# Fused backward of a linear-attention and a grouped-KV attention block: dK and dV in two shared PSUM banks, dK on eight array tiles

## The chip, the core and the metric

One core of a Trainium2 chip runs the whole kernel in one launch. The metric is the device time of that launch in microseconds. Five engines work side by side, each through its own instructions in order: TensorE (PE, with its weight loads listed apart as PEld), VectorE (DVE), ScalarE (ACT), GpSimd (POOL) and SyncE (SP, which here only issues DMAs).

## The reference, cut to what matters

Two attention blocks, A (linear attention) and B (softmax attention with one key/value head shared by 16 query heads), run forward on 2048 tokens of width 448; their outputs are concatenated, and the gradients of all inputs are taken against `grad_out`. The change is in block B:

```python
q = (x @ wq).reshape(B, S, H, Dh).transpose(0, 2, 1, 3)     # 16 heads, Dh = 28
k = x @ wk ; v = x @ wv                                     # one head each
scores = einsum("bhqd,bkd->bhqk", q, k) * Dh ** -0.5
p = softmax(scores) ; o = einsum("bhqk,bkd->bhqd", p, v)
out = o.reshape(B, S, H * Dh) @ wo
```

Its backward needs, for each head, dV = pᵀ dO, dP = dO vᵀ, dS = p ∘ (dP − rowsum), dQ = dS k and dK = dSᵀ q. Since all heads share k and v, dK and dV are sums over all 16 heads and all 2048 queries: one accumulator each, open from the first block of queries to the last.

## The kernel before

Phase A computes block A forward and backward and projects block B's q, k and v. Then the core, which the change touches, does block B's attention forward and backward in one loop over units `u` (L905). Work is cut into 64 blocks `b` (a block is 256 queries of a pair of heads), each into 8 units `tp` (256 of the 2048 keys). A unit handles its 256 keys as two halves `t2`, two heads `h`. Stages of one block run at different lags behind each other, all written out by hand inside the loop, so the order on each engine is the order of the code. In what follows r is `u % 8`. Unit u issues:

- `rows_SD` (L663): the score matmuls S of unit u into two of three rotating score banks `SB`, and the dP matmuls of unit w = u − 16 into the two banks `DB`. Each matmul uses 32 rows and all 128 columns of the array (the form 32\*128), 256 columns of moving data, eight matmuls a unit. The four dP matmuls wait for the readers of the `DB` banks of the unit before.
- on ACT: exp of the first head's scores (L927), the copy `cp` of the second head's dP out of PSUM (L941), exp of the second head's scores (L973). On DVE: dS of the first head (L939) and, for unit u − 18, a 32x32-block transpose of dS into `dsx` (L1006). On POOL: dS of the second head from `cp` (L942).
- in even units, `o_dq`: 16 matmuls that accumulate o (unnormalised output) and dQ in the bank `oq` (form 128\*32: 128 rows, 32 columns, four side by side), around them the small work of a block (the output projection `out_proj` in r = 0, transposes `onat_T` in r = 2, `don_T` in r = 6), and `dv_mm` (L875): groups of four matmuls of 512 columns into `dv_acc`, one group in r = 2 and r = 6, two in r = 4.
- in odd units, `dk_m` (L840) four times: each is four matmuls on the four diagonal 32x32 tiles of the array, tile (32a, 32a), 512 columns each, into rows 32a of `dk_acc`. Row block `a` holds group `a` of every 128 keys (32 keys each), and nothing is summed across row blocks.

Every 4th unit SP issues a DMA transpose of the exponentials (L975), which `dv_mm` later reads.

PSUM has eight banks: three `SB`, one `dv_acc` (it takes the place of a phase-A bank from u = 1 on), two `DB`, `oq` and `dk_acc`. Until u = 25, `dk_acc` also serves the projection `do_proj`/`do_copy` (L882, L891) of `grad_out`. After the loop, `dv_acc` and `dk_acc` are copied to `dkvT` (L1023 to L1031), from which the pad rows (L1069), dK's and dV's projections and the gradients of wk and wv follow.

The PE order of an odd unit followed by an even one is thus S/dP, dK, S/dP, o/dQ (with dV), and each change of form is a change of the array's tiling.

Of the kernel before, what the change touches and what calls it, by code (L numbers as in the profile page):

```python
# [8 lines left out]
ACT = mybir.ActivationFunctionType  # L9
ALU = mybir.AluOpType  # L10
AX = mybir.AxisListType
BF16 = mybir.dt.bfloat16
F32 = mybir.dt.float32
# [4 lines left out]
P = 128  # L18
# [7 lines left out]
def kernel(  # L26
# [21 lines left out]
    nc = tc.nc  # L48
    S = A_x.shape[1]
    NS = S // P  # L50
    NQC = S // 512
    scale = float(DH) ** -0.5
# [27 lines left out]
    def mm(out_ap, lhsT, rhs, start=True, stop=True):  # L80
        nc.tensor.matmul(out_ap, lhsT=lhsT, rhs=rhs, start=start, stop=stop, tile_position=(0, 0))  # L81
# [521 lines left out]
    def q_shift(pn, shift, tmp):  # L603
        a = tmp[0][0:H, :]
        nc.scalar.activation(out=a, in_=pn[0:H, :], func=ACT.Identity, bias=eps[:, 0:1], scale=kmax2[:, 0:1])
        i32 = mybir.dt.int32
        nc.vector.tensor_scalar(out=a.bitcast(i32), in0=a.bitcast(i32), scalar1=1, scalar2=None, op0=ALU.logical_shift_right)
        nc.vector.tensor_scalar(out=shift, in0=a, scalar1=1.004 * 2.0 ** 63.5, scalar2=None, op0=ALU.mult)
# [10 lines left out]
    psA = psc.enter_context(tc.tile_pool(name="psA", bufs=4, space=bass.MemoryType.PSUM))  # L619
# [7 lines left out]
    NB = 64  # L627
    NU = NB * 8
    qT_B = [R1[:, g, :] for g in range(4)]
    vaug, kn, do_nat = vaug_, kn_, R2x[:, 0:NS, :]  # L630
    with ExitStack() as cs_:
# [8 lines left out]
        pp_ = cs_.enter_context(tc.tile_pool(name="cout", bufs=2, side="right"))  # L640
        SB = [psA.tile([P, 512], F32, name="aacc") for i in range(3)]
        DB = [psA.tile([P, 512], F32, name="agen") for i in range(2)]
        oq, dk_acc = (psA.tile([P, 512], F32, name="agen") for _ in range(2))

        dsT, dsx, qX, don, doT, rl, prod = ({} for _ in range(7))
        ETs = [pe_.tile([P, 4, 2, 512], BF16, name=f"eT{i}") for i in range(5)]
# [5 lines left out]
        def eN(b, c):  # L652
            return ENs[(2 * b + c // 2) % 6][:, 16 * (c % 2):16 * (c % 2) + 16, :]

        def mmt(out, lhsT, rhs, pos, start, stop):
            nc.tensor.matmul(out, lhsT=lhsT, rhs=rhs, start=start, stop=stop, tile_position=pos,  # L656
                             skip_group_check=True)

        def blk(b):
            qc, pair = divmod(b, 8)  # L660
            return qc, pair, pair // 2, pair % 2
# [26 lines left out]
        woTp, gbT = R4, R2.rearrange("p t (c k) -> p t c k", k=P)  # L688
# [151 lines left out]
        def dk_m(b, m):  # L840
            qc, pair, g, hp = blk(b)
            h, B, s = m // 8, (m // 2) % 4, m % 2
            for a in range(4):
                rhs = dsx[b][32 * a:32 * a + 32, :, h, :, :].rearrange(
                    "p u t (b i s) -> p u t b i s", b=4, s=2)[:, :, :, B, :, s]
                mmt(dk_acc[32 * a:32 * a + 32, :],
                    qX[qc][32 * a:32 * a + 32, B, s, pair * 64 + 32 * h:pair * 64 + 32 * h + 32],
                    rhs, (32 * a, 32 * a), b == 0 and m == 0, b == NB - 1 and m == 15)

        def o_mm(v):  # L850
            b, tp = divmod(v, 8)
# [16 lines left out]
        def o_dq(vs, ys):  # L868
            for v, y in zip(vs, ys):
                todo = [f(i) for f, i in ((o_mm, v), (dq_mm, y)) if 0 <= i < NU]  # L870
                for _ in range(2):
                    for g_ in todo:
                        next(g_)

        def dv_mm(dv_acc, b, h, qb):  # L875
            for c in range(4):
                rhs = eN(b, c).rearrange("p (u h t q) k -> p u h t q k", u=2, h=2,
                                                       t=2)[:, :, h, :, qb, :]
                mmt(dv_acc[32 * c:32 * c + 32, :], don[b][:, qb, h, :], rhs, (0, 32 * c),
                    b == 0 and h + qb == 0, b == NB - 1 and h + qb == 2)  # L880

        def do_proj(i, c0, c1, ps):  # L882
            for c in range(4):
                if c1 - c0 == 512:
                    mm(ps[:, :], gbT[:, i, c, :], woTp[:, c, :], start=(c == 0), stop=(c == 3))
                    continue
                for j in range(4):
                    js = slice(32 * j, 32 * j + 32)
                    mmt(ps[js, 0:c1 - c0], gbT[:, i, c, js], woTp[:, c, c0:c1], (0, 32 * j), c == 0, c == 3)

        def do_copy(i, c0, c1, ps):  # L891
            nc.vector.tensor_copy(out=do_nat[:, i, c0:c1], in_=ps[:, 0:c1 - c0])

        do_slots = {2 * i + 1: (i, 0, 512) for i in range(13)}
        do_slots.update({32 + 8 * n: (13 + n // 4, n % 4 * P, n % 4 * P + P) for n in range(12)})
        with tc.manual_schedule():
# [8 lines left out]
            for u in range(NU + 28):  # L905
# [3 lines left out]
                b0, b1, spare = ((SB[i] for i in ((0, 1, 2), (0, 2, 1), (1, 0, 2), (1, 2, 0))[u % 4]) if hasS else SB)  # L909
# [10 lines left out]
                    out_proj(*op, spare)  # L920
                dpj = do_slots.pop(u, None)
                if dpj is not None:
                    dps_ = DB[u // 2 % 2] if u < 16 else dk_acc if u < 27 else spare
                    do_proj(*dpj, dps_)

                if hasS:
# [1 line left out]
                if u == 1:  # L928
                    q_shift(pn3, shifts[3], [pd_.tile([P, 2, 512], BF16, name="dsT").rearrange("p a b -> p (a b)").bitcast(F32)
                                             for _ in range(1)])  # L930
                    dv_acc = psA.tile([P, 512], F32, name="aacc")
                if u == 11:
                    for n in (2, 3):
                        put_shift(nc.sync, shifts[n], slice(n * 512, n * 512 + 512))
# [21 lines left out]
                if (b := due(u, 27)) is not None:  # L956
                    qc, pair, g, hp = blk(b)
                    nc.vector.tensor_scalar(out=qT_B[g][64 * hp:64 * hp + 64, qc * 256:(qc + 1) * 256],  # L958
                                            in0=oq[64:128, 0:256], scalar1=scale, scalar2=None, op0=ALU.mult)
# [10 lines left out]
                if dpj is not None:  # L970
                    do_copy(*dpj, dps_)
# [8 lines left out]
                if u % 2:  # L980
                    b, i = divmod(u - 27, 8)
                    if 0 <= b < NB:
                        for m in range(2 * i, 2 * i + 4):
                            dk_m(b, m)
                else:
                    o_dq((u - 1,), (u - 19,))
                    b, n = divmod(u - 20, 8)
                    for k in {0: (0, 1), 2: (2,), 6: (3,)}.get(n, ()) if 0 <= b < NB else ():
                        dv_mm(dv_acc, b, k // 2, k % 2)
                y = u - 18  # L990

                if 512 <= u < 530 and u % 2 == 0:
# [9 lines left out]
                if 0 <= y < NU:  # L1002
                    b, tp = divmod(y, 8)
                    if tp == 0:
                        dsx[b] = px_.tile([P, 8, 2, 2, 256], BF16, name="dsx")
                    nc.vector.transpose(  # L1006
                        out=dsx[b][:, tp, :, :, :].rearrange("p h t c -> p (h t c)").bitcast(F32),
                        in_=dsT[y][:, :, :].rearrange("p h c -> p (h c)").bitcast(F32))

        dkvT, wqT, xb = post["dkvT"], post["wqT"], post["xb"]  # L1010
# [4 lines left out]
        def gen(i, dt=F32):  # L1015
            gens[i % 2] += 1
            t = [SB, DB][i % 2][gens[i % 2] % (3 - i % 2)]
            return t.bitcast(dt) if dt != F32 else t
# [2 lines left out]
            return pd_.tile([P, 2, 512], BF16, name="dsT")[:, 0, :]  # L1021

        for c in range(4):  # L1023
            nc.vector.tensor_copy(out=dkvT[32:64, c * 512:(c + 1) * 512], in_=dv_acc[32 * c:32 * c + 32, :])
        for c in range(4):
            t = dkvT[0:32, :].rearrange("p (t a i) -> p t a i", a=4, i=32)[:, :, c, :]
            src = dk_acc[32 * c:32 * c + 32, :].rearrange("p (t i) -> p t i", i=32)
            if c % 2:
                nc.vector.tensor_scalar(out=t, in0=src, scalar1=scale, scalar2=None, op0=ALU.mult)
            else:  # L1030
                nc.scalar.activation(out=t, in_=src, func=ACT.Copy, scale=scale)  # L1031

        def dwq(c):
            r = DC_ROWS[c]
# [44 lines left out]
        for c in range(4):  # L1079
            r = DC_ROWS[c]  # L1080
            ps = gen(0)
            for st in range(NS):
# [3 lines left out]
                                 func=ACT.Copy)  # L1086
# [35 lines left out]
```

## Time and profile before

| | us |
|---|---|
| median of three runs | 1066.51 (1065.31 to 1067.93) |
| profiled execution | 1067.99 |
| its span, first to last instruction | 1066.3 |
| first exp (L927) to last, 512 units | 220.0 to 990.6 |
| mean unit between u = 40 and u = 500 | 1.512 |

| engine | busy us | share of the span |
|---|---|---|
| PE | 1042.2 | 98% |
| DVE | 896.1 | 84% |
| ACT | 873.7 | 82% |
| POOL | 781.3 | 73% |

A row of a group names line, engine, operation, output and inputs by the program's names, their shapes, the count, then busy time in us, the mean of one in ns, and the engine's idle time before them. L656 is the line of the helper `mmt`, so its groups are told apart by the tiles: `agen<-dsx,qX` is dK, `aacc<-eN,don` is dV, `agen<-doT,R` is dP, `aacc<-R,R` 32\*128 is S, `agen<-eT,R` is o and `agen<-dsT,R` is dQ. A row of the timeline gives the start, the length from the first start to the last end of what it merges, and the count. The ends of matmuls are modelled, and matmuls overlap.

### The profile page before, as it was taken

The numbers are of one execution on the slowest core, as the hardware profiler recorded it, in microseconds if no ns is written. First come the engines' busy times: TensorE is split into PE (matmuls) and PEld (weight loads), VectorE is DVE, ScalarE is ACT, GpSimd is POOL, SyncE is SP. The second block draws the span as 40 slices with busy tenths as digits, with TensorE's granted clock in tenths as the row PEclk, the third lists the DMA queues.
The fourth block names the chain that finished last, engine by engine and source line by source line (L and its number), as shares of the span: only waits on it lengthen the run. The fifth ranks groups of instructions, "written<-read, shape, count | busy, mean of one in ns | idle before, by whom it ended". The sixth has DMA issues, their size and how long they took to land.

```text
span 1066.3 us, 39861 instructions
## 1 busy us (share of the span) xinstructions
PE 1042.2 (98%) x16241; PEld 476.1 (45%) x16241; DVE 896.1 (84%) x1797; ACT 873.7 (82%) x1741; POOL 781.3 (73%) x1033
## 2 busy tenths in 40 slices
PE   9999999999999999999999999999999999999998
PEld 5555555433444444444444444444444444444434
DVE  7888400459999999999999999999999999999943
ACT  6454122479999999999999999999999999999622
POOL 6001242227988898899889989988998999888881
PEclk9999999999999999999999999999999999999999
DMA  9749899079999999999999999999999999999963
GB/s 267 163 95 200 161 214 250 21 138 168 192 202 198 170 203 187 195 191 193 196 186 189 197 192 198 185 191 194 195 195 195 195 191 186 206 191 179 218 141 92
DMA packets 689936, 195.14 MB, mean 183 GB/s; under 512 B 670616, under 2 KB 687792, under 8 KB 689752
## 3 DMA queue, kind: packets, MB, share of 16 engines
q1 hardware_dynamic: 680152, 179.92, 99.2%
q0 software_dynamic: 4640, 8.71, 2.8%
q10 hardware_dynamic: 4960, 3.96, 1.3%
q8 instruction: 127, 2.08, 0.7%
q14 instruction: 57, 0.47, 0.1%
HBM read 12.60 MB, written 10.84 MB: 22 GB/s over the span
## 4 chain that ended last, share of the span: by engine, by line
PE 52%; DVE 35%; POOL 4%; issue 4%; ACT 3%; DMA 1%; DVEq 0%; POOLq 0%; ACTq 0%
PE agen L656 20%; PE agen L81 15%; DVE dsT L939 14%; DVE dsx L1006 12%; PE aacc L656 9%; PE aacc L81 7%; POOL dsT L942 4%; DVE R L958 2%; DVE oTs L801 2%; DVE oTs L955 2%; ACT cp L941 1%; DVE rl L800 1%; ACT eT L973 1%; DMA dsx<-R 1%; ACT eT L927 0%
## 5 line engine op out<-in xcount | busy, mean ns | idle before, releaser
L942 POOL TENSOR_TENSOR dsT<-cp,eT 128x512 bf16<-128x512 bf16 x512 | 588.1, 1157 | 77.3 <-ACT cp L941 68.9
L1006 DVE STREAM_TRANSPOSE dsx<-dsT 128x512 f32<-128x512 f32 x512 | 356.4, 696 | 2.4 <-POOL dsT L942 0.2
L656 PEld LDWEIGHTS <-R 32*128 32x128 bf16 (+1 forms) x9104 | 215.5, 93 | 318.3 <-issue 293.0
L939 DVE TENSOR_TENSOR dsT<-agen,eT 128x512 bf16<-128x512 f32 x512 | 338.5, 661 | 11.7 <-PE agen L656 8.4
L941 ACT ACTIVATE cp<-agen 128x512 bf16<-128x512 f32 x512 | 324.7, 634 | 12.5 <-PE agen L656 12.5
L927 ACT ACTIVATE eT<-aacc 128x512 bf16<-128x512 f32 x512 | 324.0, 633 | 11.6 <-PE aacc L656 4.7
L973 ACT ACTIVATE eT<-aacc 128x512 bf16<-128x512 f32 x512 | 330.6, 646 | 0.0
L656 PE MATMUL agen<-doT,R 32*128 32x256 bf16 x2048 | 270.9, 269 | 10.9 <-DVE dsT L939 8.2
L656 PE MATMUL aacc<-R,R 32*128 32x256 bf16 (+1 forms) x2240 | 269.7, 268 | 2.7 <-ACT eT L927 0.8
L656 PE MATMUL agen<-dsx,qX 32*32 32x512 bf16 x4096 | 267.7, 375 | 0.0
L656 PE MATMUL agen<-eT,R 128*32 128x256 bf16 x2048 | 182.0, 276 | 0.1
L656 PE MATMUL agen<-dsT,R 128*32 128x256 bf16 x2048 | 181.4, 276 | 0.1
L656 PEld LDWEIGHTS <-qX 32*32 32x32 bf16 x4096 | 79.7, 89 | 114.9 <-issue 54.3
L656 PE MATMUL aacc<-eN,don 128*32 128x512 bf16 x1024 | 97.6, 379 | 0.0
L81 PEld LDWEIGHTS <-R 128*128 128x128 bf16 (+1 forms) x517 | 41.0, 99 | 42.9 <-issue 11.1
L406 POOL COPY pk<-R 128x256 bf16<-128x256 bf16 x4 | 1.6, 397 | 75.3 <-DVE R L366 75.3
L81 PE MATMUL agen<-R,R 128*128 128x448 bf16 (+1 forms) x180 | 42.4, 363 | 0.3 <-ACT R L225 0.3
L833 POOL COPY qst<-R 128x512 bf16<-128x512 bf16 x56 | 34.2, 611 | 4.8 <-DMA qX<-qst 4.6
L805 POOL TENSOR_TENSOR prod<-R,oTs 128x128 f32<-128x128 bf16 x64 | 27.5, 430 | 9.8 <-DVE oTs L801 9.8
L656 PEld LDWEIGHTS <-don 128*32 128x32 bf16 x1024 | 34.2, 97 | 0.8
L422 DVE TENSOR_TENSOR osb<-aacc,pr 64x448 bf16<-64x448 f32 x2 | 1.2, 617 | 37.9 <-DMA out_dram<-osb 24.0
L958 DVE TENSOR_SCALAR R<-agen 64x256 bf16<-64x256 f32 x64 | 27.3, 426 | 3.6 <-PE agen L656 1.6
(231 smaller groups left out, 971.1 us busy)
## 6 DMA issues: line engine op xcount, KB each, us to landing
out_dram<-osb ACTq DMA_DIRECT2D x22, 112.0 KB
eN<-eT SPq DMA_TRANSPOSE x128
xa<-in_A_x_dram SPq DMA_DIRECT2D x8, 224.0 KB
ga<-in_grad_out_dram SPq DMA_DIRECT2D x4, 448.0 KB
xa<-in_grad_out_dram POOLq DMA_DIRECT2D x4, 448.0 KB, 5.7
out_dram<-wdq POOLq DMA_DIRECT2D x8, 224.0 KB, 3.8
eT<-in_grad_out_dram SPq DMA_DIRECT2D x4, 448.0 KB
eT<-in_B_x_dram SPq DMA_DIRECT2D x4, 448.0 KB
```

The lines of the kernel that those rows point to most:

```text
L81: nc.tensor.matmul(out_ap, lhsT=lhsT, rhs=rhs, start=start, stop=stop, tile_position=(0, 0))
L656: nc.tensor.matmul(out, lhsT=lhsT, rhs=rhs, start=start, stop=stop, tile_position=pos, skip_group_check=True)
L801: nc.vector.tensor_tensor(out=os_, in0=onp[:, :, :, :], in1=r_[:].to_broadcast([P, 2, 2, 32]), op=ALU.mult)
L805: nc.gpsimd.tensor_tensor(out=prod[b][:], in0=dnv, in1=os_, op=ALU.mult)
L833: eng.tensor_copy(out=st.rearrange("p (b s) a j -> p b s a j", s=2)[:, :, s, :, :], in_=src.unsqueeze(2).to_broadcast([P, 4, 4, 32]))
L927: nc.scalar.activation(out=eT(u)[:, 0, :], in_=sp[0][:, :], func=ACT.Exp, scale=scale)
L939: nc.vector.tensor_tensor(out=dst[:, 0, :], in0=dp[0][:, :], in1=ew[:, 0, :], op=ALU.mult)
L941: nc.scalar.activation(out=cp[:, :], in_=dp[1][:, :], func=ACT.Copy)
L942: nc.gpsimd.tensor_tensor(out=dst[:, 1, :], in0=cp[:, :], in1=ew[:, 1, :], op=ALU.mult)
L958: nc.vector.tensor_scalar(out=qT_B[g][64 * hp:64 * hp + 64, qc * 256:(qc + 1) * 256], in0=oq[64:128, 0:256], scalar1=scale, scalar2=None, ...
L973: nc.scalar.activation(out=eT(u)[:, 1, :], in_=sp[1][:, :], func=ACT.Exp, scale=scale)
L1006: nc.vector.transpose(out=dsx[b][:, tp, :, :, :].rearrange("p h t c -> p (h t c)").bitcast(F32), in_=dsT[y][:, :, :].rearrange("p h c -> p ...
```

## The change

dK and dV no longer have a bank each: both banks hold dK in columns 0 to 255 and dV in columns 256 to 511, each for half of the keys (n = 0, 1). A dK step issues eight matmuls of 256 columns in place of four of 512: for each row block `a`, one on tile (32a, 32a) into bank 0 and one on tile (32a, 32((a+1) mod 4)) into bank 1. A dV group becomes eight matmuls of 256 columns in place of four of 512. So that dK's accumulation can start without a clearing flag beside dV's, dV's first block (b = 0) is issued whole in u = 26, after the last `do_proj` in these banks; `do_proj` and `do_copy` of u = 17 to 25 work in two halves. The copies after the loop are 16 of 256 columns in place of 8 of 512. The order of everything else is as it was.

```diff
-        oq, dk_acc = (psA.tile([P, 512], F32, name="agen") for _ in range(2))
+        oq, acc0 = (psA.tile([P, 512], F32, name="agen") for _ in range(2))
+        kv_acc = [acc0]
...
             for a in range(4):
                 rhs = dsx[b][32 * a:32 * a + 32, :, h, :, :].rearrange(
                     "p u t (b i s) -> p u t b i s", b=4, s=2)[:, :, :, B, :, s]
-                mmt(dk_acc[32 * a:32 * a + 32, :],
-                    qX[qc][32 * a:32 * a + 32, B, s, pair * 64 + 32 * h:pair * 64 + 32 * h + 32],
-                    rhs, (32 * a, 32 * a), b == 0 and m == 0, b == NB - 1 and m == 15)
+                for n in range(2):
+                    j = 32 * ((a + n) % 4)
+                    mmt(kv_acc[n][j:j + 32, 0:256],
+                        qX[qc][32 * a:32 * a + 32, B, s, pair * 64 + 32 * h:pair * 64 + 32 * h + 32],
+                        rhs[:, 4 * n:4 * n + 4], (32 * a, j), False, b == NB - 1 and m == 15)
...
-        def dv_mm(dv_acc, b, h, qb):
-            for c in range(4):
...
-                mmt(dv_acc[32 * c:32 * c + 32, :], don[b][:, qb, h, :], rhs, (0, 32 * c),
-                    b == 0 and h + qb == 0, b == NB - 1 and h + qb == 2)
+        def dv_mm(b, h, qb):
+            for n in range(2):
+                for c in range(4):
+                    rhs = eN(b, c).rearrange("p (u h t q) k -> p u h t q k", u=2, h=2, t=2)[:, n, h, :, qb, :]
+                    mmt(kv_acc[n][32 * c:32 * c + 32, 256:512], don[b][:, qb, h, :], rhs, (0, 32 * c),
+                        b == 0 and h + qb == 0, b == NB - 1 and h + qb == 2)
...
-                    for k in {0: (0, 1), 2: (2,), 6: (3,)}.get(n, ()) if 0 <= b < NB else ():
-                        dv_mm(dv_acc, b, k // 2, k % 2)
+                    for k in ({0: (0, 1), 2: (2,), 6: (3,)} if b else {6: range(4)}).get(n, ()) if 0 <= b < NB else ():
+                        dv_mm(b, k // 2, k % 2)
...
         for c in range(4):
-            nc.vector.tensor_copy(out=dkvT[32:64, c * 512:(c + 1) * 512], in_=dv_acc[32 * c:32 * c + 32, :])
+            for n in range(2):
+                nc.vector.tensor_copy(out=dkvT[32:64, c * 512 + n * 256:c * 512 + n * 256 + 256],
+                                      in_=kv_acc[n][32 * c:32 * c + 32, 256:512])
```

More of the change, by code (lines that the diff above doesn't have):

```diff
@@ L873, in o_dq @@
                         next(g_)
-        def dv_mm(dv_acc, b, h, qb):
-            for c in range(4):
-                rhs = eN(b, c).rearrange("p (u h t q) k -> p u h t q k", u=2, h=2,
-                                                       t=2)[:, :, h, :, qb, :]
-                mmt(dv_acc[32 * c:32 * c + 32, :], don[b][:, qb, h, :], rhs, (0, 32 * c),
-                    b == 0 and h + qb == 0, b == NB - 1 and h + qb == 2)
-        def do_proj(i, c0, c1, ps):
+        def dv_mm(b, h, qb):
[4 more added lines that the diff above has]
+                        b == 0 and h + qb == 0, b == NB - 1 and h + qb == 2)
+        def do_proj(i, c0, c1, ps):
+            if ps is None:
+                for n in range(2):
+                    for c in range(4):
+                        mm(kv_acc[n][:, 0:256], gbT[:, i, c, :], woTp[:, c, 256 * n:256 * n + 256], start=(c == 0), stop=(c == 3))
+                return
             for c in range(4):
@@ L891, in do_copy @@
         def do_copy(i, c0, c1, ps):
+            if ps is None:
+                for n in range(2):
+                    nc.vector.tensor_copy(out=do_nat[:, i, 256 * n:256 * n + 256], in_=kv_acc[n][:, 0:256])
+                return
             nc.vector.tensor_copy(out=do_nat[:, i, c0:c1], in_=ps[:, 0:c1 - c0])
@@ L922 @@
                 if dpj is not None:
-                    dps_ = DB[u // 2 % 2] if u < 16 else dk_acc if u < 27 else spare
+                    dps_ = DB[u // 2 % 2] if u < 16 else None if u < 27 else spare
                     do_proj(*dpj, dps_)
@@ L930 @@
                                              for _ in range(1)])
-                    dv_acc = psA.tile([P, 512], F32, name="aacc")
+                    kv_acc.append(psA.tile([P, 512], F32, name="aacc"))
                 if u == 11:
@@ L1023 @@
         for c in range(4):
-            nc.vector.tensor_copy(out=dkvT[32:64, c * 512:(c + 1) * 512], in_=dv_acc[32 * c:32 * c + 32, :])
+            for n in range(2):
+                nc.vector.tensor_copy(out=dkvT[32:64, c * 512 + n * 256:c * 512 + n * 256 + 256],
+                                      in_=kv_acc[n][32 * c:32 * c + 32, 256:512])
         for c in range(4):
[L1026 to L1031, printed above, removed]
+            for n in range(2):
+                t = dkvT[0:32, n * S // 2:(n + 1) * S // 2].rearrange("p (t a i) -> p t a i", a=4, i=32)[:, :, c, :]
+                j = 32 * ((c + n) % 4)
+                src = kv_acc[n][j:j + 32, 0:256].rearrange("p (t i) -> p t i", i=32)
+                if c % 2:
+                    nc.vector.tensor_scalar(out=t, in0=src, scalar1=scale, scalar2=None, op0=ALU.mult)
+                else:
+                    nc.scalar.activation(out=t, in_=src, func=ACT.Copy, scale=scale)
         def dwq(c):
```

## The prediction, made before the changed kernel was run

> **What bounds the kernel now.** I read the engine table first, then the chain's shares, then the groups of the steady loop, and then the timeline of single units, which overturns the first two.
>
> ```profile
> PE 1042.2 (98%) x16241; PEld 476.1 (45%) x16241; DVE 896.1 (84%) x1797; ACT 873.7 (82%) x1741; POOL 781.3 (73%) x1033
> ...
> PE 52%; DVE 35%; POOL 4%; issue 4%; ACT 3%; DMA 1%; DVEq 0%; POOLq 0%; ACTq 0%
> ```
>
> PE looks like the bound: busy 98%, 52% of the chain. But ends of matmuls are modelled, and a PE that waits in the middle of a burst still counts as busy. The groups of the loop (300 to 1000 us, by form; 463 units):
>
> ```profile
> L1006 DVE STREAM_TRANSPOSE dsx<-dsT 128x512 f32<-128x512 f32 x463 | 322.3, 696 | 2.2 <-POOL dsT L942 0.2
> L939 DVE TENSOR_TENSOR dsT<-agen,eT 128x512 bf16<-128x512 f32 x463 | 306.0, 661 | 7.4 <-PE agen L656 4.3
> ...
> L941 ACT ACTIVATE cp<-agen 128x512 bf16<-128x512 f32 x463 | 294.5, 636 | 3.7 <-PE agen L656 3.6
> ...
> L656 PE MATMUL agen<-dsx,qX 32*32 32x512 bf16 x3700 | 241.9, 375 | 0.0
> ```
>
> ACT runs three operations a unit. They start 0.477 us apart, and without a pause each ends 12 to 13 ns later after its start than the one before, so ACT's real pace is 0.49 us: 1.47 us a unit, of a mean unit of 1.512. DVE has about 1.42 us of starts a unit. There is at most (1.512 − 1.47) x 512 = 21 us to gain, whatever PE does. Now the pair of units 249 (r = 1) and 250 (r = 2): PE's timeline, and of ACT's the copy `cp` of unit 249.
>
> ```profile
> 594.16 1.05 PE L656 MATMUL agen<-dsx,qX 32*32 32x512 bf16 x16
> 595.14 0.28 PE L656 MATMUL aacc<-R,R 32*128 32x256 bf16 x2
> 595.15 0.28 PE L656 MATMUL agen<-doT,R 32*128 32x256 bf16 x1
> 595.26 0.27 PE L656 MATMUL aacc<-R,R 32*128 32x256 bf16 x2
> 595.27 0.43 PE L656 MATMUL agen<-doT,R 32*128 32x256 bf16 x3
> 595.63 0.29 PE L656 MATMUL agen<-eT,R 128*32 128x256 bf16 x2
> ```
>
> ```profile
> 594.55 0.72 ACT L941 ACTIVATE cp<-agen 128x512 bf16<-128x512 f32 x1
> ```
>
> dK ends and S/dP of unit 250 start at 595.14. But the last two dP matmuls write the bank that `cp` of unit 249 reads until 594.550 + 0.725 = 595.275. The first starts 0.051 later, the second 0.108 after it, and the o/dQ phase 0.195 after that: 595.629, 0.354 after the end of `cp`. I took this distance for every even unit of some 60 blocks. It is 0.354 at the median for r = 0, 2, 4 and 6 alike; its mean lies above that by 0.003 (r = 0), 0.009 (2), 0.029 (4) and 0.000 (6). **So the end of `cp`, not the end of dK, starts nearly every o/dQ phase.** dK ends 0.136, 0.136, 0.020 and 0.095 before `cp` (medians). Since the waiting dP can issue 0.03 after S/dP starts, dK could be longer by 0.157, 0.157, 0.041 and 0.116 before o/dQ moved.
>
> What costs the 0.5 us a block in which ACT idles, then? Two loops without dK. From exp to exp, r = 1 to r = 3: `cp` starts 0.478 after the exp and takes 0.725; 0.354 to o/dQ; o/dQ with `onat_T` and a dV group lasts 1.148; the second S matmul 0.12 later, the exp 0.304 after it: 3.129, which is what the trace has (594.072 to 597.201; ACT alone needs 2.87). Then DVE's burst of small work, r = 1 to 4:
>
> ```profile
> 597.46 0.65 DVE L939 TENSOR_TENSOR dsT<-agen,eT 128x512 bf16<-128x512 f32 x1
> 598.14 0.42 DVE L958 TENSOR_SCALAR R<-agen 64x256 bf16<-64x256 f32 x1
> 598.49 0.70 DVE L1006 STREAM_TRANSPOSE dsx<-dsT 128x512 f32<-128x512 f32 x1
> 599.21 0.69 DVE L939 TENSOR_TENSOR dsT<-agen,eT 128x512 bf16<-128x512 f32 x1
> ```
>
> DVE has no pause here; the dP matmul of unit 253 waits for the end of this last L939 (599.90) and starts at 599.956, while PE had come to that phase 0.33 earlier. The next exp is at 600.276.
>
> **The change, part by part.** *dK, removed and added.* Today four steps of 0.217 and 0.31 from the last start to the next phase: 0.976. In a set, loads and matmuls alternate every 3.2 ns, so a set of eight tiles is issued 0.045 after its first matmul. Sets of 256 columns follow each other by 0.109 in o/dQ, and from the last start of such a set to the next phase it is 0.20. New dK phase: 0.045 + 3 x 0.109 + 0.20 = 0.57, if tiles that share 32 rows, or 32 PSUM partitions of different banks, overlap. Both halves are seen: o/dQ starts four tiles on the same rows, with four moving operands, 3 ns apart; S and dP from different rows go to the same partitions of two banks, 3 to 4 ns apart. Saved: 0.40 an odd unit, some 97 us of PE time over 243. What hides it: `cp`. In the units where dK decides now, the shortening is worth the means above: r = 0 and 2 give 0.012 a block. r = 4's 0.029 I leave out, since L939 holds the phase after it by 0.35. 0.012 x 60 = **−0.7 us**. Bounds: 0, and 7.6 us if every block (mean 12.092 from exp to exp, r = 5 to 5) came to the shortest, 11.965.
>
> A page speaks against the change. Row first: in o/dQ, weights for rows that are all in use load while those rows stream:
>
> ```profile
> 601.71 0.12 PEld L656 LDWEIGHTS <-R 128*32 128x32 bf16 x8 [0.21 <-issue]
> 601.72 0.29 PE L656 MATMUL agen<-eT,R 128*32 128x256 bf16 x2
> ```
>
> Eight loads are through 0.12 after the first, with the 0.29 us matmuls in flight. The Trainium skill ("TensorE: Matmul & The Clock Gate", What overlaps and what doesn't) says that loads overlap running matmuls only on other row groups. By that the second rival below would come about in place of this sum: 1121 us or more in place of 1066. The row decides, for 128\*32; no row shows it for two tiles of a row group in 32\*32.
>
> *dV.* Two sets of 512 columns (0.216 apart, 0.312 to the next phase) become four of 256 (0.109, 0.205): 0.528 against 0.532; one group 0.312 against 0.314. In r = 2 it is on the path: 0.002 x 60 = **+0.1**.
>
> *Order and waits.* POOL and SP keep their order; ACT gains two and DVE eleven instructions, all of them copies told of below. PE gains 5140 load and matmul pairs; no new wait stands in dK or dV. PE fetches instructions in blocks of 16 KB (0.95 us each, one per 6.3 us now, one per 5 then); no PE gap lies at a fetch now: nothing, or some us if one came late.
>
> *Start.* Five 512-column `do_copy`s (0.576 to 0.69) become pairs of 256 (0.33 each, after L955): +0.09 x 5. dV of block 0 moves three groups of 0.216 from u = 20 and 22, units of 1.94 and 1.90, to u = 26, one of 1.45: between −0.65 and +0.65, taken as 0. Together **+0.4**.
>
> *Tail.* From u = 512 PE is nearly without gaps, and thirteen dK phases lie there. But:
>
> ```profile
> 1032.00 1.05 PE L656 MATMUL agen<-dsx,qX 32*32 32x512 bf16 x16
> 1032.98 1.69 PE L81 MATMUL aacc<-eT,R 128*128 128x448 bf16 x8
> 1035.34 0.38 PE L81 MATMUL aacc<-dsx,eT 128*128 128x448 bf16 x1 [0.68 <-DMA dsx<-R]
> ```
>
> PE ends by waiting for four DMA transposes into a `dsx` buffer, which one after another take from 1020.60 to 1035.3. They start when dK of u = 529 has ended (1020.54). So only savings up to there count: 0.40, and 0.13 each in the odd units 521 to 527 (L939 ends 0.18 before the next dP, 0.05 of it the hand-over): 0.9. Later, `dx` needs pad rows that land at 1043.57, after a row of DMA issues on POOL without a gap, 0.36 before their use. I take half, **−0.5** (bounds 0 and 0.9). The last copies (four dK copies take 2.65 now, some 0.4 more after) lie under PE's work and the transposes.
>
> Sum: −0.7 + 0.1 + 0.4 − 0.5 = −0.7. Against the profiled execution 1067.99 − 0.7 = 1067.3; this execution lies 1.5 above the median of the runs, so 1066.51 − 0.7 = 1065.8.
>
> **The rivals.** What a measurement of this kernel can tell from no change is about 0.3%, 3.2 us.
>
> *Faster, PE was the bound.* For it: 98%, and the chain through dK at units like 253. Against it: the 0.354. All blocks at the shortest gives 1066.5 − 7.6 − 0.9 = 1058; at ACT's pace 1066.5 − 21 = 1046. Chance 0.24.
>
> *Slower, a load waits for the matmul on its rows.* A row group then does its eight loads (0.088 each) and matmuls (0.109) one after another: 8 x 0.197 = 1.58 a phase, longer by 0.60. It decides from 0.976 + 0.157 = 1.13 on: o/dQ starts 0.60 − 0.157 = 0.44 later in r = 0 and 2, and ACT waits each time: 0.89 x 62 blocks = 55 us, 1121; with r = 4 and 6 on the path too (0.56 and 0.48), 120 us. A phase of 1.16, from smaller hitches, costs 0.03 x 2 x 62 = 3.7: 1070. For it: no row shows two tiles of a row group in 32\*32. Against: the loads at 601.71. Chance 0.14, half of it for the mild form.
>
> *It does not do what it says.* Tiles of a row group take turns: 8 x 0.109 + 0.1 = 0.97, dK as long as now, 1066.5. Chance 0.12.
>
> **How the numbers follow.** dK at half its length and no change beyond 0.3%: 0.50. With the third rival, 0.62 within 0.3%; faster 0.24, slower 0.14. Range: 1057 leaves out a tenth, the deeper half of the faster case; 1070 leaves out the heavy slower case and a little of the mild one.
>
> **What would show it.** Right: dK phases of 0.57, o/dQ still 0.354 after `cp`, PE standing before the dP matmuls; ACT's idle time a block still 0.5 us. Wrong: a mean block below 11.95 us (a wait that I took for fixed was not), or dK above 1.13.

## The result, and the profile after

The changed kernel takes 1164.81 us (median of 4 runs, 1161.55 to 1170.13) against 1066.74 (4 runs, 1065.31 to 1067.93): 1.0925 of the time before, 95% interval 1.0882 to 1.0968. It is 98 us slower, far outside the range on record. The profiled execution took 1164.69, its span is 1163.0; from the first exp to the last it has 866.7 us, where the kernel before has 770.6. So the loop has all of the loss.

The engines' line and the chain of the page after, to be read against the two lines that the prediction opens with:

```profile
PE 1050.3 (90%) x21381; PEld 544.8 (47%) x21381; DVE 904.5 (78%) x1808; ACT 878.6 (76%) x1743; POOL 784.5 (67%) x1033
...
PE 50%; DVE 24%; issue 12%; ACT 8%; POOL 3%; DMA 1%; DVEq 0%; ACTq 0%; POOLq 0%
```

No engine has more work worth the name (PE and DVE 8 us more each); what has grown is `issue`, from 4% of the chain to 12%: time in which the engine waited for nothing that the profile shows. Two further lines of the page, the granted clock in 40 slices and the queue that brings instructions. Before:

```profile
PEclk9999999999999999999999999999999999999999
...
q8 instruction: 127, 2.08, 0.7%
```

After:

```profile
PEclk9999999999898999899988887989999989999999
...
q8 instruction: 167, 2.74, 0.9%
```

Each of these packets holds 16 KB, and 2 x 21381 loads and matmuls by 167 packets make 256 instructions in one: what PE executes comes in instruction blocks of 256 (not to be taken for the blocks of queries), and there are now 40 more of them.

The loop's groups (300 to 1100 us, by form; busy, mean ns, then idle time and its releasers):

```profile
L1018 DVE STREAM_TRANSPOSE dsx<-dsT 128x512 f32<-128x512 f32 x467 | 325.6, 697 | 2.0 <-DVE doT L830 0.2
L951 DVE TENSOR_TENSOR dsT<-agen,eT 128x512 bf16<-128x512 f32 x466 | 310.3, 666 | 62.8 <-PE agen L657 59.2
...
L953 ACT ACTIVATE cp<-agen 128x512 bf16<-128x512 f32 x466 | 296.2, 636 | 11.2 <-PE agen L657 10.2 <-POOL qst L834 1.0
...
L657 PE MATMUL aacc<-dsx,qX 32*32 32x256 bf16 x3732 | 171.0, 289 | 30.6 <-issue 30.5
```

DVE and ACT need the same for each operation as before, and now wait for PE. PE waits for `issue`, 30.5 us of it ahead of dK, whose instructions have no data to wait for in the middle of a phase. One such place, PE's timeline at 547 us:

```profile
547.65 0.28 PE L657 MATMUL agen<-dsT,R 128*32 128x256 bf16 x2
547.75 0.32 PE L657 MATMUL aacc<-wo,R 128*32 128x112 bf16 x11
549.86 0.37 PE L657 MATMUL aacc<-wo,R 128*32 128x112 bf16 x5 [1.79 <-issue]
```

A group of 16 equal matmuls with one pair of operands stops after eleven, and five follow 1.79 us later. The view of DMA traffic in 547 to 551 us (slices of 0.1 us):

```profile
DMA  9820500000000000001899999999999999999999
...
q1 hardware_dynamic: 1949, 0.49, 66.1%
q8 instruction: 1, 0.02, 1.5%
```

The packets of the `eN` DMA transpose (q1) thin out and end at 547.41; the one instruction packet (the 5 in the fifth slice) starts at 547.40, where they end, and is through at 548.34; PE goes on at 549.86. I numbered all of PE's records in the order of their starts: loads, matmuls and the 31 of its sequencer. In the loop, counted from 245 us on, there are 65 gaps of over 0.6 us between two successive starts at index 193 modulo 256, 1.44 us on average, 93 us in all, and each ends 1.2 to 2.3 us (median 1.4) after an instruction packet has landed. Only three gaps over 0.6 us lie elsewhere, all before 255 us. The kernel before has none at this index. So the work looks as fast as forecast, with PE running out of instructions; the experiments test this.

### The profile page after: what moved, and what is told of

Same layout as the page of the kernel before. It is cut to its first block, busy times and chain, and to the rows that moved or that the text cites. A ratio compares the mean times of both kernels' runs of the same rounds, so it can differ in the third digit from the quotient of the medians.

```text
span 1163.0 us, 50155 instructions
## 1 busy us (share of the span) xinstructions
PE 1050.3 (90%) x21381; PEld 544.8 (47%) x21381; DVE 904.5 (78%) x1808; ACT 878.6 (76%) x1743; POOL 784.5 (67%) x1033
## 4 chain that ended last, share of the span: by engine, by line
PE 50%; DVE 24%; issue 12%; ACT 8%; POOL 3%; DMA 1%; DVEq 0%; ACTq 0%; POOLq 0%
PE agen L657 19%; PE agen L81 13%; PE aacc L657 12%; DVE dsT L951 10%; DVE dsx L1018 9%; PE aacc L81 5%; ACT cp L953 5%; ACT eT L985 2%; POOL dsT L954 2%; DVE R L970 1%; PE aacc L792 1%; DVE oTs L802 1%; ACT eT L939 1%; DVE oTs L967 1%; POOL out_dram L780 1%
## 5 line engine op out<-in xcount | busy, mean ns | idle before, releaser
L657 PEld LDWEIGHTS <-R 32*128 32x128 bf16 (+1 forms) x9104 | 235.5, 95 | 338.8 <-issue 308.4
L657 PE MATMUL agen<-doT,R 32*128 32x256 bf16 x2048 | 299.7, 283 | 29.6 <-DVE dsT L951 14.3
L657 PE MATMUL aacc<-R,R 32*128 32x256 bf16 (+1 forms) x2240 | 297.9, 281 | 7.0 <-issue 4.4
L657 PE MATMUL aacc<-dsx,qX 32*32 32x256 bf16 x4096 | 186.3, 288 | 31.9 <-issue 31.8
L657 PE MATMUL agen<-dsT,R 128*32 128x256 bf16 x2048 | 197.0, 291 | 9.2 <-issue 5.6
L657 PE MATMUL agen<-dsx,qX 32*32 32x256 bf16 x4096 | 186.6, 288 | 0.0
L657 PE MATMUL aacc<-eN,don 128*32 128x256 bf16 x1024 | 84.3, 291 | 7.1 <-issue 7.1
L657 PE MATMUL agen<-eN,don 128*32 128x256 bf16 x1024 | 84.1, 292 | 2.5 <-issue 2.5
L657 PEld LDWEIGHTS <-don 128*32 128x32 bf16 x2048 | 66.4, 104 | 16.1 <-issue 11.5
L81 PE MATMUL agen<-R,R 128*128 128x448 bf16 (+2 forms) x180 | 40.2, 350 | 0.4 <-ACT R L225 0.4
```

## Theories

*A, instruction supply.* When PE enters an instruction block, the fetch of the next is due, but it starts, as a rule, only where a running transpose's packets end (116 of the 147 fetches in the changed kernel's loop start within 0.3 us of a transpose's last packets; of random moments 22% lie so near). In the kernel before the wait is 0 to 4.1 us (median 2.0) and the fetch 0.95; the packet was there 1.81 us before PE needed it at the least, and in the changed kernel's gaps a start takes at least 1.2 from the landing. In the kernel before 256 instructions last 6.7 us (median), after the change 4.9 where nothing stops. *B, the clock.* A shorter dK leaves PE idle, the granted clock is halved, and that is the loss: it is at 0.5 in 24 stretches of the loop, 122.9 us, and in none before. *D* (fetches are late whatever else moves) and *E* (the shared banks or the halved dV cost the time) came up on the way.

## The experiments

Stalls below are gaps at the instruction blocks' place, counted as above; "clock" is the mean granted clock of the profiled execution.

**dK on four tiles again, with as many instructions.** Both halves on tile (32a, 32a); the copies at the end read them there, so dK is complete, and what the expectation says of wrong places does not hold.

```diff
-                    j = 32 * ((a + n) % 4)
+                    j = 32 * a
```

> The changed kernel with every dK matmul put on the diagonal tiles (row group 32a to column group 32a, for both halves n), so that the two matmuls of a row group share one tile and take turns; dK's rows are therefore summed in the wrong places. The instruction count, their order and every DMA stay as in the changed kernel, and dK's phase goes back to about one microsecond (0.98 before). Theory A (instruction supply: TensorE now uses up its 256-instruction blocks faster than the fetches, which start only where the 5.5 us DMA transpose stream ends, bring them): the stalls at one fixed place of every 256 instructions stay, 40 to 70 of them of about 1.5 us, and the time stays above 1120 us. Theory B (the shorter dK leaves TensorE idle, the granted clock falls to a half, and that is what costs the time): with dK long again the mean granted clock is back at about 0.99 and the time at 1060 to 1080 us.

1175.64 us, 1.1021 [1.0997, 1.1044]; dK 1.00 us at the median; 58 stalls, 86 us; clock 0.974, 58 us at half clock. A held. The dK phase is as long as before, PE is busy for 1075.7 us, longer than in either kernel, and the time is 11 us longer than after the change with half of its time at half clock: the loss goes neither with a short dK nor with the lowered clock, and the stalls stay. Why it is 11 us longer with 7 us less of stalls was not taken apart.

**Transposes cut in two,** in the changed kernel and in the kernel before.

```diff
-                    if u % 4 == 3:
-                        nc.sync.dma_start_transpose(ENs[u // 4 % 6][:, :, :],
...
+                    if u % 2 == 1:
+                        a0 = u % 4 - 1
+                        nc.sync.dma_start_transpose(ENs[u // 4 % 6][:, 8 * a0:8 * a0 + 16, :],
...
```

> The changed kernel with each eN DMA transpose of four units cut into two of two units each, issued at every second unit; the same bytes, nothing left out. Theory A (fetches wait for the running transpose): the stream that a fetch waits behind is about half as long, so the wait falls from up to 4.2 us to about 2 us, the stalls go from about 65 to below 15, the granted clock returns to about 0.99, and the time is 1055 to 1080 us. Theory B (idle TensorE lowers the clock): the TensorE work is the same as in the changed kernel, so the time stays at 1150 to 1170 us. If a cut transpose is no shorter (a fixed cost each), A too expects no gain, which the length of its stream will show.

> The kernel before with the same cut of the eN transposes into two; the control for what the cut itself costs. Both theories: no stalls of TensorE at the block's place before or after the cut, so the time stays at 1062 to 1072 us, unless the two short transposes together take longer than the one long one, which would show as later O and dV steps and a time above 1075 us.

1432.53 us and 1441.25 us. A's and B's times were missed; what came is the proviso of the control, that the two short transposes take longer than the long one (above 1075 us). The changed kernel's page and chain say why:

```profile
PE 37%; DMA 21%; ACT 19%; POOL 8%; issue 7%; DVE 7%; SPq 1%; ACTq 0%; DVEq 0%; POOLq 0%
DMA eN<-eT 21%; PE agen L657 11%; PE agen L81 11%; ACT cp L953 10%; PE aacc L657 8%; ACT eT L985 7%; POOL dsT L954 7%; PE aacc L81 5%; DVE dsT L951 3%; DVE dsx L1019 3%; SPq L838 1%; ACT eT L939 1%; POOL qst L834 0%; SPq L988 0%; PE aacc L85 0%
```

A half transpose's packets last 2.6 to 3.0 us instead of 5.1 to 5.5, but one is issued per 4.50 us on average (300 to 1200 us), where one whole transpose per 6.05 (four units of 1.512) served before: two units now take 4.5 us, and dV waits for `eN` (50 waits, 238 us, between 300 and 1200 us). As a test of the time it is void, as the control shows. One thing can be read: the wait of a fetch falls to 0.8 us (median) from 3.15, and no stall at the instruction blocks' place is left; but 256 instructions last longer here too (5.7), so that this alone does not decide.

**Half of dK's steps left out of the kernel before.**

```diff
-                            dk_m(b, m)
+                            if m % 2 == 0 or m == 15:
+                                dk_m(b, m)
```

> The kernel before without the dK steps of odd m (m = 15 stays): half of dK's sums are left out, so dK's phase is about as short as after the change (0.5 us instead of 0.98), and TensorE idles as long in each unit, but with fewer instructions than before (about 200 pairs of load and matmul per 8 units instead of 230; the changed kernel has 310). Theory A: no stalls, clock about 0.99, time 1040 to 1068 us (not faster than the end of the copy cp allows). Theory B: the same idle time gives the same lowered clock, 0.94 to 0.95, and a time above 1120 us.

1066.90 us, 0.9997 [0.9986, 1.0008]; dK 0.545; no stall; clock 0.998. A held, B fell in its plain form. It is also the forecast's mechanism by itself: take 0.43 us from three of four dK phases, and about half of that from the fourth, and nothing happens to the time.

**The changed kernel without the transposes,** which all instructions stay in.

```diff
-                    if u % 4 == 3:
+                    if u % 4 == 3 and u < 24:
                         nc.sync.dma_start_transpose(ENs[u // 4 % 6][:, :, :],
```

> The changed kernel without the eN transposes from unit 24 on: dV is summed from stale data, and nothing waits for eN any more. Every TensorE instruction stays, in its order. Theory A (instruction fetches wait for the end of the 5 us transpose stream, and TensorE runs out of instructions): with no stream to wait behind, a fetch follows its request at once (below 1 us instead of 3 us in the middle case), no stall at the block's place is left of about 65, the granted clock is about 0.99, and the time is 1055 to 1070 us. Rival D (the fetches are late whatever else moves: 0.95 us each plus a fixed delay): the stalls stay, 40 to 70 of them, and the time stays above 1130 us. Theory B (idle TensorE lowers the clock): the same, above 1130 us, with a clock near 0.95.

1063.39 us, 0.9959 [0.9946, 0.9971]. The page:

```profile
PE 1016.2 (96%) x21375; PEld 545.0 (51%) x21381; DVE 892.2 (84%) x1808; ACT 870.9 (82%) x1743; POOL 781.9 (74%) x1033
...
PEclk9999999999999999999999999999999999999999
...
q8 instruction: 167, 2.74, 1.1%
...
DVE 46%; PE 30%; ACT 9%; issue 7%; POOL 7%; DVEq 0%; DMA 0%; ACTq 0%; POOLq 0%
```

The same 167 instruction blocks, no stall, a full clock, and the 98 us are gone. A fetch waits 0.6 us (median), and is there 1.6 us ahead at the least. D and E fall with this run, and B too as the cause of this loss: all of PE's work on its eight tiles, and PE idle wherever it is ahead, kept the clock.

**The same cut in the kernel before.**

> The kernel before without the eN transposes from unit 24 on (dV is summed from stale data), the control for the same cut in the changed kernel, which gave 1063.4 us. If the change itself gains when it has its instructions in time (rival: TensorE was the bound in part), this run stays at 1066 to 1069 us and the changed kernel without transposes is ahead by 3 to 5 us. If the change is worth nothing even then, as the forecast's sum had it, and the 4 us come from the missing transposes, this run is at 1062 to 1065 us too.

1065.95 us, 0.9981 [0.9972, 0.9991] of the kernel before. That lies between what the two cases expected. So the missing transposes are worth about 2 us, and 0.9959 / 0.9981 = 0.998, again some 2 us, is left for the change itself if it has its instructions in time (by the two intervals, 2 give or take 2): below what the prediction set as its bound of no change.

**Instructions alone, in doses.** In the kernel before, each dK step of odd m below 15 is replaced by 2, 3 or 4 rounds of four matmuls of 4 columns: less PE work, more instructions, nothing else of the change. The diff is that of four rounds.

```diff
-            for a in range(4):
+            for a in [0, 1, 2, 3] * (4 if m % 2 and m < 15 else 1):
...
+                if m % 2 and m < 15:
+                    rhs = dsx[b][32 * a:32 * a + 32, 0, h, 0, 0:4]
-                mmt(dk_acc[32 * a:32 * a + 32, :],
+                mmt(dk_acc[32 * a:32 * a + 32, 0:4] if m % 2 and m < 15 else dk_acc[32 * a:32 * a + 32, :],
```

> The kernel before, where each dK step of odd m below 15 is replaced by two rounds of four matmuls of 4 columns (part of dK's sums is wrong for that): less TensorE work than before, and about 258 pairs of load and matmul in 8 units instead of 230. Theory A: 256 instructions last about 5.9 us, somewhat less than the worst case of wait, fetch and start (4.2 + 0.95 + 1.4 us): 3 to 25 stalls, time 1067 to 1100 us. Without theory A there is no reason for any: 1062 to 1069 us.

> The step between two doses already run: each dK step of odd m below 15 replaced by three rounds of four matmuls of 4 columns, about 286 pairs of load and matmul in 8 units (part of dK's sums is wrong for that). 258 pairs gave 5 stalls and 1070 us, 314 gave 60 stalls and 1182 us. Theory A (late instruction fetches): 256 instructions last some 5.4 us, so that each fetch that has to wait longer than about 3.1 us ends in a stall, which in the kernel before would have been 3 in 10 of them: 25 to 50 stalls of some 0.5 to 1.5 us and 1085 to 1140 us, with the clock below 0.99. Without theory A: 1062 to 1072 us.

> The kernel before, where each dK step of odd m below 15 is replaced by four rounds of four matmuls of 4 columns (part of dK's sums is wrong for that): less TensorE work than before, no shared banks, no change to dV, and about 314 pairs of load and matmul in 8 units, as many as after the change (310). Theory A: the same stalls as after the change, 45 to 75, and a time of 1130 to 1190 us. Rival E (the new layout costs the time) and B (the idle time of TensorE does it; half of the dK steps alone left out gave no loss): 1060 to 1075 us.

| kernel | instruction blocks | stalls (sum, us) | at half clock, us | first to last exp | time, median |
|---|---|---|---|---|---|
| before, half dK | 113 | 0 | 0 | 769.3 | 1066.90 |
| before | 127 | 0 | 0 | 770.6 | 1066.74 |
| two rounds | 141 | 5 (4) | 0 | 775.1 | 1069.87 |
| three rounds | 155 | 40 (52) | 58 | 826.4 | 1121.67 |
| after | 167 | 65 (93) | 123 | 866.7 | 1164.81 |
| four rounds | 169 | 60 (96) | 140 | 886.2 | 1182.45 |

Ratios: 1.0015 [1.0001, 1.0030], 1.0509 [1.0469, 1.0548], 1.1068 [1.1012, 1.1124]. All three lie in what A expected, and without A the last two should have been some 50 and over 100 us faster; for two rounds the time alone could not tell, its five stalls do. The kernel before stands at the edge: by the ratios 11% more instructions cost some 2 us, 22% some 54. The loss in the loop is about the sum of the stalls: 56 for 52, 96 for 93, 116 for 96. What the half clock behind them adds was not separated.

**The changed kernel with part of its dK steps,** m = 0, 4, 8, 12, 15, and then even m and 15.

```diff
-                            dk_m(b, m)
+                            if m % 4 == 0 or m == 15:
+                                dk_m(b, m)
```

> The changed kernel with 5 of 16 dK steps (m = 0, 4, 8, 12, 15); the rest of dK's sums is left out. The shared banks, the eight tiles, the dV halves and every DMA stay; the pairs of load and matmul fall from about 310 to 222 in 8 units, below the 230 of the kernel before. Theory A: hardly a stall at the block's place (at most 5), clock 0.99, time 1058 to 1070 us, which is the time that the change would have had with enough instructions. Rival E (something else in the new layout, such as the shared banks or the halved dV, costs the time): above 1120 us. Theory B (idle TensorE lowers the clock): the idle time is greater still, so above 1120 us at a clock of 0.95 or less.

> The changed kernel with 9 of 16 dK steps (even m and 15; the rest of dK's sums is left out): about 254 pairs of load and matmul in 8 units, and more TensorE work than the run with 5 of 16 steps, which had no stalls but hundreds of us at half clock and 1121 us. Theory A with the clock as a second, separate effect of too little TensorE work: at most 15 stalls, and the clock either full, with 1062 to 1075 us, or lowered for long stretches without stalls ahead of them, with 1080 to 1130 us; the kernel before with half its dK steps, at the same share of busy TensorE (0.96), kept its clock, which speaks for the first. Rival E (the new layout itself costs time): above 1100 us at a full clock.

With 9 of 16 steps (139 blocks) 1074.25 us, 1.0063 [1.0028, 1.0097], two stalls and 3.4 us at half clock in the profiled execution (1071.51): as expected, and E falls again. Its eight executions spread from 1068 to 1083 us at granted clocks of 0.997 to 0.976, so some lowered clock is here too. With 5 of 16 (123 blocks) there is no stall, as expected, but A's time was missed, and E and B, which said above 1120 us, came nearer: three executions took 1117 to 1124 us at granted clocks of 0.89 to 0.91 (1.0479 [1.0434, 1.0525]), the profiled one 1209 at 0.754. Three windows of the latter, the only one with a trace (us; then busy PE, PEld, DVE, ACT, POOL; PEclk, DMA share, GB/s):

```profile
290.00:294.90 4.90, 3.99 (x69) 1.86 (x71) 3.94 (x9) 4.36 (x9) 4.90 (x5) 1.00 1.11 224
294.90:455.00 160.10, 159.95 (x2236) 66.61 (x2231) 126.06 (x233) 122.92 (x243) 112.97 (x136) 0.50 0.90 149
456.00:462.00 6.00, 5.42 (x103) 2.48 (x103) 5.70 (x12) 6.00 (x14) 4.43 (x4) 1.00 1.16 193
```

So a halved clock without any stall at the instruction blocks' place exists, once dK is cut to a third: B names something real, at less work than the change leaves. What ends such a stretch, here after 160 us, stays open.

**What the lowered clock is in the changed kernel.** Around the longest stall of the first hundred us of the loop (columns as above):

```profile
303.80:307.20 3.40, 3.40 (x107) 1.80 (x103) 3.19 (x7) 3.36 (x8) 3.40 (x5) 1.00 1.20 238
307.20:310.60 3.40, 0.83 (x28) 0.35 (x25) 1.25 (x3) 1.18 (x4) 1.77 (x2) 1.00 1.29 163
310.60:314.00 3.40, 3.40 (x69) 1.48 (x69) 2.69 (x6) 2.54 (x6) 2.19 (x4) 0.50 1.52 211
314.00:317.40 3.40, 3.29 (x88) 1.84 (x88) 3.37 (x7) 3.40 (x9) 2.76 (x4) 1.00 0.71 136
```

The stall comes first, at full clock; the half clock follows for 3.4 us. All stretches at half clock in this kernel's loop last 3.4 us or two or three times that. All 21 falls of the clock up to 950 us, lined up on this grid, follow a window in which PE was busy for 0.25 to 0.73 of the time (median 0.56; the other windows' median is 0.96), and the 20 of them that lie in the loop follow a stall. The share alone does not decide: 13 other windows at full clock, busy for 0.59 to 0.73, had no fall behind them. The Trainium skill ("TensorE: Matmul & The Clock Gate", What's actually happening) has the clock halved after an idle window of about 3.4 us. The length of the window agrees; here a window that was busy up to 0.73 could be enough.

## Why the prediction was wrong

*The step that failed* is the last sentence of "Order and waits". It had the rate after the change right (one instruction block per 5 us; 4.9 measured) and the one before a little fast (6.3; the trace has 6.7), and priced the fetch at "nothing, or some us if one came late", because no PE gap lay at a fetch. That reads a term that is hidden as a term that is free. That the margin was gone could be read in the trace of before: the wait was up to 4.1 us, behind a transpose that runs most of the time, and with 0.95 for the fetch that is 5.05, more than the 5 that the block was to last. With the 1.2 to the start, which only the changed kernel's trace shows, it is 6.2 against 4.9. A wait over 2.75 us makes a block late by this sum, and 34% of the waits of before were longer; after the change 65 of the 147 instruction blocks in the loop were late. Measured: 93 us of stalls for a term of zero, and none of the rivals had it; the two marks named as wrong, a mean block below 11.95 us or dK above 1.13, did not come either: the mean block of eight units is 13.75, and dK has 0.58 at the median (of the 33 phases above 1.13 in the loop, 30 hold a stall).

*dK.* Right: a phase of 0.565 to 0.59 us (medians) against 0.57 forecast, in the eight tiles that share rows and PSUM partitions. The second rival's reason and "does not do what it says" are refuted by it, and with it, for 32\*32, the page's rule that loads overlap only matmuls on other row groups.

*Where the saving goes.* Right: half of dK less gave 0.9997. In the changed kernel without transposes o/dQ starts 0.354 after the end of `cp` at r = 0, 2, 4 and 6 (medians), on average 0.354, 0.354, 0.383 and 0.354, and a block takes 12.063 us; the kernel before without transposes has 12.072 (12.090 with them). That is 0.009 a block or 0.5 us in 60, where the sum had 0.7. So the means above 0.354 at r = 0 and 2 vanished, as worked out. The one at r = 4, which the sum left out, stayed with dK at half its length, so it was not dK's; whose it is was not looked into.

*dV, start, tail* were not taken apart by a run of their own; together with dK they are within the 2 us that the two kernels without transposes leave between them. The first rival, PE as the bound, would have shown there as 8 us or more and did not.

## What to carry to other kernels

Count instructions as a resource: the number of 256-instruction blocks, the time in which PE uses one up, and against it the longest wait of a fetch, its length and the start. Halving the columns of a matmul doubles its instructions, and a long DMA on the same DMA engines can decide how early the next block comes. A term that is hidden has a margin, and the margin is to be compared with what the change takes from it.

## What the runs showed of the hardware that was not expected

A 16 KB instruction fetch of 0.95 us as a rule waits for the end of a running DMA transpose's packets, up to 4.6 us, and PE, where it stands for it, goes on no earlier than 1.2 us after it has landed. The Trainium skill ("Trainium Architecture — The Big Picture", The software stack) has the instruction streams copied into each engine when the kernel is loaded. That is not the whole of it: in the kernels here 113 to 169 blocks for PE come while the kernel runs. Cutting each DMA transpose in two made two come in 9.0 us, where the whole one came in the 6.05 that four units take; what fills the 1.5 to 1.9 us between one half's packets and the next one's was not looked into. And TensorE can stay at half clock for 85 to 198 us with its records busy throughout (159.95 of 160.10 us above), where the changed kernel's falls last 3.4 to 10.2.
